# Attention and routed feed-forward on one core: routing's small operands and q's norms move to PSUM, first squares to ScalarE, whole dense chunks, and a tail written out by hand

## The chip, the cores and the metric

The kernel runs on one core of a Trainium2 chip. The metric is the device time of one execution in microseconds (us). The core has TensorE (PE in the profile; its weight loads are PEld), VectorE (DVE), ScalarE (ACT), GpSimd (POOL) and SyncE (SP), which run their own instruction streams and wait for one another by semaphores. Tiles lie in SBUF or in PSUM, the memory into which TensorE's results go; PSUM has eight banks of 2 KB in each partition here.

## What is computed

Attention with RMS-normalised q and k over 8 batches, 12 heads, 448 tokens and 64 channels; its result, seen as 3584 tokens of 768 channels, goes through a dense feed-forward layer and, added to it, one of eight expert layers, chosen per token by the largest gate logit and weighted by its probability.

```python
q_n, k_n = (rmsnorm(q, g_q), rmsnorm(k, g_k))       # x / sqrt(mean(x*x) + 1e-6) * g
attn = np.exp(scores)                               # scores = q_n k_n^T / 8, less the row's maximum
attn = attn / (np.sum(attn, axis=-1, keepdims=True) + 1e-09)
return np.matmul(attn, v).astype(np.float32)
...
h_dense = np.maximum(x @ w1_dense, 0.0)
y_dense = h_dense @ w2_dense
logits = x @ w_gate
expert_idx = np.argmax(logits, axis=1)
...
    h = np.maximum(x[mask] @ w1[e], 0.0)
    y_moe[mask] = gate_w[mask, None] * (h @ w2[e])
return (y_dense + y_moe).astype(np.float32)
```

## The kernel before

The program has two phases. The first (up to L478) does attention, routing and the first dense layer; the second (from L480) gathers tokens by expert and does the rest in 35 tiles of up to 128 tokens.

In the first phase the 96 heads go in 24 groups of four, three groups to a batch. `load` (SP queue) fetches q and k of a group, `load_v` (POOL queue) fetches v of two groups. `squares` (L183, POOL) squares q and k, `sums` (L188, DVE) adds over the channels, `norms` (L194, ACT) makes mean squares into reciprocal roots by Ln and Exp, `normalise` (L200) multiplies, q on DVE and k on POOL, `transposes` (L208, PE) and `turned` (L216, DVE) bring them channel-first. `scores` (L226) does four matmuls and one large Exp on ACT, seven times a group; the Exp's results lie in the tail of the expert weights' tile `we`, so the last weights load late. `attend` (L240) multiplies by v, 28 small matmuls for each of four steps, `divide` (L256, DVE) normalises into `xa`, `xtrans` (L265, PE) and `xturned` (L275, DVE) transpose that into `xT`.

Per batch, routing follows: `logits` (L279, PE), `choose` (L288, DVE: maximum, differences `cent`, the first maximal expert as `hot` and one-hot `oh`; ACT's Exp; the gate value; stores to `records`, a DRAM tensor with one row per token), `ranks` (L313, PE: how many earlier tokens chose each expert), and `places` (L325, DVE): it adds the counts so far, keeps the chosen expert's number in `rf`, splits it in whole tiles `tj` and rest `lo` through int32 and a shift (L335 to L338), and makes the selection matrix `sel`. The first dense layer is made in chunks of six matmuls of 512 columns, one chunk for 128 tokens: `fill` (L437) issues them a few at a time, `dense` (L346) writes a bank `ff`, `relu` (L356, ACT) empties it into `hd` and SP stores that to `records`. `hd` has one buffer.

PSUM: two buffers of two banks for scores, and four one-bank buffers that `tr`, `av`, `xt`, `lp`, `rk` and `ff` take in turn, in the order in which the program asks for them.

The order of the instructions on PE, POOL, SP, DVE and ACT is that of the code (`manual_schedule`, L447). `period(g)` (L370) is one turn: around the seven scores of group g+1 it puts the attention of group g, the normalising and transposing of group g+2 and the squares, sums and norms of group g+3; the transposes of x of group g-1 at the end; and, when a batch's second group is under way, the routing of the batch before. Weights go out on POOL's queue at a pace (`LATE`, `WPACE`, at i == 2).

After the loop come the rest of the dense chunks, then the second phase's table of slots on DVE (L490 to L550: `tl` compares slot numbers with tile numbers, `val` multiplies by token numbers), 32 matmuls `slp` (L517), and the first gathers (L555).

Of the kernel before, what the change touches and what calls it, by code (L numbers as in the profile page):

```python
# [9 lines left out]
F32 = mybir.dt.float32  # L10
BF16 = mybir.dt.bfloat16
# [7 lines left out]
def kernel(  # L19
# [71 lines left out]
    lo = const.tile([P, B, 4], BF16)  # L91
# [6 lines left out]
    LATE, WPACE = 8, 2.6  # L98
# [36 lines left out]
    with tc.tile_pool(name="a_ld", bufs=2) as ld, \  # L135
# [3 lines left out]
        xin, sqs, ssqs, rs, xn, qkT, exs, xas, xTs, avs, trs = [{} for _ in range(11)]  # L139
# [41 lines left out]
        def squares(g, name):  # L181
            for hh in range(2):
                sqs[name, g, hh] = sb.tile([P, J * D], F32, tag="sq", name="sq", bufs=3)  # L183
                x = xin[name, g][:, hh]
                nc.gpsimd.tensor_mul(sqs[name, g, hh], x, x)  # L185
# [14 lines left out]
        def normalise(g, name):  # L200
            eng = nc.vector if name == "q" else nc.gpsimd
# [63 lines left out]
        def xtrans(g):  # L265
            b, gb = divmod(g, NPR // GP)
            ps = wkp.tile([P, GP, S], BF16, tag="wk", name="xt")
# [5 lines left out]
            trs["x"] = ps  # L273

        def xturned(g):  # L275
            b, gb = divmod(g, NPR // GP)
            nc.vector.tensor_copy(xTs[b][:, gb * GP:(gb + 1) * GP], trs["x"])  # L277

        def logits(b):  # L279

            lp = wkp.tile([P, 4, E], F32, tag="wk", name="lp")
# [4 lines left out]
            trs["l"] = lp  # L286

        def choose(b):  # L288
            lp = trs["l"]
            mx = sb.tile([P, 4, 1], F32, tag="mx")  # L290
            nc.vector.tensor_reduce(mx, lp, AX.X, ALU.max)
            cent = sb.tile([P, 4, E], F32, tag="cent")
            nc.vector.tensor_sub(cent, lp, mx.to_broadcast([P, 4, E]))

            hot = sb.tile([P, 4, E], F32, tag="hot")
# [8 lines left out]
            nc.scalar.activation(eg, cent, AF.Exp)  # L304
            sm = sb.tile([P, 4, 1], F32, tag="sm")
            nc.vector.tensor_reduce(sm, eg, AX.X, ALU.add)
# [6 lines left out]
        def ranks(b):  # L313

            rk = wkp.tile([P, 5, E], F32, tag="wk", name="rk")
# [7 lines left out]
            trs["r"] = rk  # L323

        def places(b):  # L325
            rk = trs["r"]
            c0, c1 = counts[b % 2], counts[1 - b % 2]
            rr = sb.tile([P, 4, E], F32, tag="rr")
# [3 lines left out]
            rf = sb.tile([P, 4], F32, tag="rf")  # L332
# [332 lines left out]
```

## Time and profile before

| | |
|---|---|
| timed runs | 501.01, 504.06, 504.98 us |
| profiled execution | 500.06 us |
| its span in the trace | 498.4 us |
| busy PE | 398.2 us (80%), mean granted clock 0.912 |
| busy DVE | 299.1 us (60%) |
| busy POOL | 263.4 us (53%) |
| busy ACT | 234.4 us (47%) |
| read from HBM | 74.90 MB |

The span goes from the first to the last instruction; the execution's own time has 1.66 us around it. The busy shares are means over two phases that differ much: in the first DVE, POOL and ACT carry most of their work, in the second PE runs almost without a break. A line Lnnn is a line of the kernel; `y<-xq,r 128x448 bf16<-128x448 f32` is the output tile, the inputs, and their partitions, elements and types; a bracket such as `[0.82 <-ACT hd L360]` is the idle time of that engine before the row and the instruction that ended it.

### The profile page before, as it was taken

Reading aid. Unit: us, or ns where it says so; the run is one execution under the profiler, and the core shown is the slowest. Engines: PE = TensorE matmul, PEld = TensorE weight load, DVE = VectorE, ACT = ScalarE, POOL = GpSimd, SP = SyncE. Lnnn points to the kernel's source line nnn. Section 1 sums busy time; section 2 is a strip of 40 time slices with the busy share of each in tenths; the row PEclk is TensorE's granted clock in tenths of the full one; section 3 lists DMA queues with packets and bytes.
Section 4 is the critical chain, followed back from the end, with each engine's and each line's share of the span. In section 5 each row is a group of like instructions: output and inputs, shape, how many; then the busy total and the mean of one; then the engine's idle time right before and its main releaser. Section 6 shows DMA issues by size and latency. Waiting matters only on the chain.

```text
span 498.4 us, 13956 instructions
## 1 busy us (share of the span) xinstructions
PE 398.2 (80%) x5628; PEld 241.8 (49%) x5628; DVE 299.1 (60%) x747; ACT 234.4 (47%) x362; POOL 263.4 (53%) x285
## 2 busy tenths in 40 slices
PE   0448787878979859788788862499999999999994
PEld 0135463544535536545455521346666666666662
DVE  3569899998998989998984515213323323323320
ACT  1437774765846847758567102023333333333331
POOL 8689994774784947659742200304434434434422
PEclk9999897997989989989888857569999999999999
DMA  8949767498393973945649994414453454454430
GB/s 217 243 110 260 149 184 156 131 254 169 99 228 114 189 200 94 283 117 130 140 84 154 232 215 124 117 36 151 128 182 128 132 180 137 135 169 165 143 121 1
DMA packets 50303, 77.24 MB, mean 155 GB/s; under 512 B 8573, under 2 KB 46205, under 8 KB 50240
## 3 DMA queue, kind: packets, MB, share of 16 engines
q0 software_dynamic: 24544, 43.31, 39.6%
q1 hardware_dynamic: 25376, 33.04, 20.9%
q8 instruction: 46, 0.75, 0.6%
q14 instruction: 17, 0.14, 0.1%
q10 hardware_dynamic: 320, 0.00, 0.0%
HBM read 74.90 MB, written 23.86 MB: 198 GB/s over the span
## 4 chain that ended last, share of the span: by engine, by line
issue 30%; DVE 30%; POOL 14%; PE 13%; DMA 9%; ACT 2%; POOLq 1%; ACTq 0%; SPq 0%; DVEq 0%
DMA records<-hd 7%; POOL xg L555 7%; DVE ssq L190 6%; DVE xa L262 5%; PE av L253 5%; DVE y L204 4%; POOL sq L185 3%; PE sc L235 3%; POOL out_dram L609 3%; PE ff L351 3%; DVE y L221 2%; DVE xT L277 2%; DVE lo L338 2%; ACT hd L360 2%; DMA gk<-in_g_k_dram 1%
## 5 line engine op out<-in xcount | busy, mean ns | idle before, releaser
L238 ACT ACTIVATE we<-sc 128x896 bf16<-128x896 f32 x168 | 147.1, 919 | 63.9 <-PE sc L235 63.3
L609 POOL DMA_INDIRECT out_dram<-ys,dest x35 | 35.5, 1014 | 97.9 <-ACT ys L608 97.9
L253 PE MATMUL av<-va,we 64*128 64x65 bf16 x2688 | 68.0, 197 | 16.5 <-DVE xT L277 10.0
L235 PE MATMUL sc<-y 64*64 64x448 bf16 x672 | 69.5, 411 | 12.8 <-ACT we L238 11.4
L204 POOL TENSOR_TENSOR y<-xk,r 128x448 bf16<-128x448 f32 x48 | 52.3, 1110 | 41.4 <-ACT r L197 41.4
L253 PEld LDWEIGHTS <-we 64*128 64x128 bf16 x2688 | 53.1, 98 | 42.0 <-issue 38.7
L351 PE MATMUL ff<-wd,xT 128*128 128x512 bf16 x192 | 59.1, 449 | 12.6 <-DVE xa L262 9.3
L589 ACT COPY heT<-hp 128x512 bf16<-128x512 bf16 x35 | 20.5, 585 | 92.4 <-PE hp L587 89.7
L607 DVE COPY ys<-yp 128x384 f32<-128x384 f32 x35 | 19.5, 557 | 72.7 <-issue 55.7
L185 POOL TENSOR_TENSOR sq<-xk 128x448 f32<-128x448 f32 x48 | 44.2, 936 | 31.9 <-DVE ssq L190 31.6
L190 DVE TENSOR_REDUCE ssq<-sq 128x7 f32<-128x448 f32 x96 | 56.0, 609 | 4.5 <-POOL sq L185 4.3
L555 POOL DMA_INDIRECT xg<-records,row x35 | 34.2, 977 | 43.6 <-DVE t L543 32.4
L577 PE MATMUL he<-we,xT 128*128 (+1 forms) x210 | 53.6, 393 | 0.2 <-issue 0.2
L596 PE MATMUL yp<-wd,hdT 128*128 128x384 bf16 x280 | 51.2, 326 | 1.1 <-ACT ys L608 1.1
L566 DVE COPY xT<-xp 128x768 bf16<-128x768 bf16 x35 | 19.5, 557 | 53.4 <-PE he L577 30.0
L601 PE MATMUL yp<-we,heT 128*128 (+1 forms) x280 | 51.2, 326 | 0.0
L185 POOL TENSOR_TENSOR sq<-xq 128x448 f32<-128x448 f32 x48 | 49.0, 1041 | 0.0
L204 DVE TENSOR_TENSOR y<-xq,r 128x448 bf16<-128x448 f32 x48 | 46.0, 998 | 4.8 <-ACT r L197 4.8
L213 PE MATMUL tr<-ident,y 128*128 128x128 bf16 x336 | 27.3, 239 | 27.0 <-DVE y L204 22.2
L262 DVE TENSOR_TENSOR xa<-av,inv 128x256 bf16<-128x256 f32 x96 | 40.7, 424 | 3.3
L235 PEld LDWEIGHTS <-y 64*64 64x64 bf16 x672 | 20.9, 107 | 40.0 <-issue 30.6
L213 PEld LDWEIGHTS <-y 128*128 128x128 bf16 x336 | 22.5, 108 | 33.7 <-DVE y L204 23.9
(101 smaller groups left out, 497.8 us busy)
## 6 DMA issues: line engine op xcount, KB each, us to landing
we<-in_moe_w_dram POOLq DMA_DIRECT2D x16, 768.0 KB
xq<-in_q_dram SPq DMA_DIRECT2D x25, 448.0 KB, 4.2
xk<-in_k_dram SPq DMA_DIRECT2D x25, 448.0 KB, 5.2
xv<-in_v_dram POOLq DMA_DIRECT2D x11, 448.0 KB
records<-xa SPq DMA_DIRECT2D x8, 576.0 KB, 7.2
records<-hd SPq DMA_DIRECT2D x24, 128.0 KB, 1.8
wd<-in_moe_w_dense_dram POOLq DMA_DIRECT2D x2, 768.0 KB
records<-xa SPq DMA_DIRECT2D x8, 96.0 KB, 7.7
```

The lines of the kernel that those rows point to most:

```text
L185: nc.gpsimd.tensor_mul(sqs[name, g, hh], x, x)
L190: nc.vector.tensor_reduce(ssqs[g][:, "qk".index(name), hh], sqs[name, g, hh].rearrange("p (j d) -> p j d", d=D), AX.X, ALU.add)
L204: eng.tensor_mul(y[:, :, hh], xin[name, g][:, hh].rearrange("p (j d) -> p j d", d=D), rs[g][:, "qk".index(name), hh].unsqueeze(2) .to_broa ...
L235: nc.tensor.matmul(ps[r * D:(r + 1) * D, hh, :S], kT[rows, r, j], qT[rows, r].rearrange("p j s -> p (j s)"), start=True, stop=True)
L238: nc.scalar.activation(x, ps[:, :, :S], AF.Exp, scale=scale)
L253: nc.tensor.matmul(avs[hh, r][:, m], exs[g, j][rows, hh, QC[m]:QC[m] + P], va[rows, hh, j, :De], start=(j == 0), stop=(j == J - 1))
L262: nc.vector.tensor_mul(xas[b][:, :, h * D:(h + 1) * D], avs[hh, r][:, :, :D], inv.to_broadcast([P, 4, D]))
L351: nc.tensor.matmul(ff[0], xTs[b][:, kk, QC[m]:QC[m] + P], wd1[:, kk], start=(kk == 0), stop=(kk == KD - 1))
L555: nc.gpsimd.indirect_dma_start(out=xg, out_offset=None, in_=rec, in_offset=bass.IndirectOffsetOnAxis(ap=row[:, t:t + 1], axis=0))
L577: nc.tensor.matmul(he, xTs[t][:, kk], we[:, bass.ds(eregs[t], 1), 0, kk * F:(kk + 1) * F] .rearrange("p o f -> p (o f)"), start=(kk == 0), ...
L596: nc.tensor.matmul(yp[:, dd, :HD], hdTs[t][:, i], wd2[:, i, dd * HD:(dd + 1) * HD], start=(i == 0), stop=False)
L601: nc.tensor.matmul(yp[:, dd, :HD], heTs[t][:, i], we[:, bass.ds(eregs[t], 1), 1, i * Dm + dd * HD:i * Dm + (dd + 1) * HD] .rearrange("p o ...
```

## The change

- `hot`, `cent` and, in `places`, `rr`, `rf` and `lo` are no longer SBUF tiles but unused columns of the PSUM bank of `lp` or `rk`. The int32 chain becomes float arithmetic: `tj` is rounded by adding and subtracting 12582912, one instruction less.
- `norms` is one Ln and two Exps; k's norms go to SBUF, q's to the spare end of the bank that the transposes of x (`xt`) fill. `norms` now takes that bank; `xtrans` moves from the end of a period (group g-1) to i == 0 of the next (g-2), and `xturned` from i == 0 to i == 1.
- The gate value and the stores leave `choose` for a function `gates`, called after `ranks`.
- `fill` issues six matmuls, a whole chunk, instead of five, and `hd` has two buffers.
- At the start ACT squares the first two groups, DVE normalises the first group's k too, and `constants` and the first three weight loads stand after the squares of the third group. In the loop `LATE` goes from 8 to 5 and `WPACE` from 2.6 to 2.1; the last weight is loaded in the second phase, at t == 0.
- The loop runs 24 periods; its two last ones are written out, with the last batch's dense chunks between `choose` and `ranks`, and between `places` and the slot matmuls. `tl` and `val` are made in two halves.

```diff
-    LATE, WPACE = 8, 2.6
+    LATE, WPACE = 5, 2.1
...
+                if scalar:
+                    nc.scalar.activation(sqs[name, g, hh], x, AF.Square)
+                else:
+                    nc.gpsimd.tensor_mul(sqs[name, g, hh], x, x)
...
-            r = sb.tile([P, 2, 2, J], F32, tag="r", name="r")
-            nc.scalar.activation(r, ssqs[g], AF.Ln, bias=eps_t, scale=1.0 / D)
-            nc.scalar.activation(r, r, AF.Exp, scale=-0.5)
-            rs[g] = r
...
+            ln = sb.tile([P, 2, 2, J], F32, tag="ln", name="ln")
+            nc.scalar.activation(ln, ssqs[g], AF.Ln, bias=eps_t, scale=1.0 / D)
+            trs["x"] = wkp.tile([P, 1024], BF16, tag="wk", name="xt")
+            rs["q", g] = trs["x"][:, GP * S:].bitcast(F32)[:, :2 * J].rearrange(
+                "p (h j) -> p h j", h=2)
+            rs["k", g] = sb.tile([P, 2, J], F32, tag="r", name="r")
+            for n, name in enumerate("qk"):
+                nc.scalar.activation(rs[name, g], ln[:, n], AF.Exp, scale=-0.5)
...
-                               rs[g][:, "qk".index(name), hh].unsqueeze(2)
-                               .to_broadcast([P, J, D]))
+                               rs[name, g][:, hh].unsqueeze(2).to_broadcast([P, J, D]))
...
-            lp = trs["l"]
+            ws = trs["w"]
+            lp, hot, cent = [ws[:, i * 4 * E:(i + 1) * 4 * E].rearrange("p (m e) -> p m e", e=E)
+                             for i in range(3)]
...
-            cent = sb.tile([P, 4, E], F32, tag="cent")
...
-            hot = sb.tile([P, 4, E], F32, tag="hot")
...
+            rr = ws[:, 64:64 + 4 * E].rearrange("p (m e) -> p m e", e=E)
+            rf, lof = ws[:, 128:132], ws[:, 132:136]
...
-            ri = sb.tile([P, 4], I32, tag="ri")
-            nc.vector.tensor_copy(ri, rf)
-            nc.vector.tensor_scalar(ri, ri, 7, None, op0=ALU.arith_shift_right)
-            nc.vector.tensor_copy(tj[:, b], ri)
-            nc.vector.scalar_tensor_tensor(lo[:, b], in0=tj[:, b], scalar=-float(P), in1=rf,
+
+            nc.vector.tensor_scalar(lof, rf, 63.5, 1.0 / P, op0=ALU.subtract, op1=ALU.mult)
+            nc.vector.tensor_scalar(tj[:, b], lof, 12582912.0, 12582912.0, op0=ALU.add,
+                                    op1=ALU.subtract)
+            nc.vector.scalar_tensor_tensor(lof, in0=tj[:, b], scalar=-float(P), in1=rf,
...
-                hd = sb.tile([P, F], BF16, tag="hd", bufs=1)
+                hd = sb.tile([P, F], BF16, tag="hd", bufs=2)
...
-                        xturned(g - 2)
+                        xtrans(g - 2)
...
-                        fill(g, 5)
+                        fill(g, KD)
...
+                    if g > 1:
+                        xturned(g - 2)
...
-                    if g > 0 and g - 1 < NG:
-                        xtrans(g - 1)
                     if gb == 1 and g > 1:
                         ranks(b - 1)
+                        gates(b - 1)
                         places(b - 1)
-                    fill(g, 5)
+                    fill(g, KD)
...
-                constants()
                 setup()
+                for name in "qk":
+                    squares(0, name, scalar=True)
...
+                for name in "qk":
+                    normalise(0, name, nc.vector)
+                    transposes(0, name)
...
+                for name in "qk":
+                    squares(1, name, scalar=True)
...
+                for j in range(J):
+                    scores(0, j)
+                    if j == 1:
+                        norms(1)
+                        for name in "qk":
+                            normalise(1, name)
+                        squares(2, "q")
...
                 for job in wjobs[:3]:
                     nc.gpsimd.dma_start(*job)
...
+                constants()
+                norms(2)
...
+                xtrans(NG - 2)
+                xturned(NG - 2)
+                fill(NG, KD)
                 relu()
-                fill(10 ** 6, 10 ** 6)
+                xtrans(NG - 1)
+                xturned(NG - 1)
+                logits(B - 1)
+                choose(B - 1)
+                fill(NG + 1, 12)
                 relu()
-                while nw[0] < len(wjobs):
+                ranks(B - 1)
+                gates(B - 1)
+                places(B - 1)
+                fill(NG + 1, 12)
+                relu()
+                while nw[0] < len(wjobs) - 1:
...
+                if t == 0:
+                    nc.gpsimd.dma_start(*wjobs[-1])
```

Three places show how instructions stand now. The first is DVE at the end of a period with routing: `places` and what follows it, with the engines and queues that a row waits for. Before:

```order
L329 TENSOR_TENSOR rr<-rk,counts_90 128x32 [waits PE_49]
L330 TENSOR_TENSOR counts_89<-rk,counts_90 128x8
L331 TENSOR_TENSOR rr<-rr,oh 128x32 [waits DVE_49]
L333 TENSOR_REDUCE rf<-rr 128x4 [waits DVE_49]
L335 CAST ri<-rf 128x4 [waits DVE_49]
L336 TENSOR_SCALAR ri<-ri 128x4 [waits DVE_49]
L337 CAST tj<-ri 128x4 [waits DVE_49]
L338 SCALAR_TENSOR_TENSOR lo<-tj,rf 128x4 [waits DVE_49]
L340 TENSOR_TENSOR sel<-iop,lo 128x512 [waits DVE_49]
L277 COPY xT<-xt 128x896
L204 TENSOR_TENSOR y<-xq,r 128x7x64 [waits DMAHW3_49,Activation_49]
```

Of the change, the same place (`rk` names every tile that shares the bank, `xt` the bank in which q's norms lie):

```order
L344 TENSOR_TENSOR rk<-rk,counts_89 128x32 [waits PE_49]
L345 TENSOR_TENSOR counts_88<-rk,counts_89 128x8 [waits DVE_49]
L346 TENSOR_TENSOR rk<-rk,oh 128x32 [waits DVE_49]
L347 TENSOR_REDUCE rk<-rk 128x4 [waits DVE_49]
L349 TENSOR_SCALAR rk<-rk 128x4 [waits DVE_49]
L350 TENSOR_SCALAR tj<-rk 128x4 [waits DVE_49]
L352 SCALAR_TENSOR_TENSOR rk<-tj,rk 128x4 [waits DVE_49]
L354 TENSOR_TENSOR sel<-iop,rk 128x512 [waits DVE_49]
L211 TENSOR_TENSOR y<-xq,xt 128x7x64 [waits DMAHW2_49,PE_49,Activation_49]
...
L285 COPY xT<-xt 128x896
```

One instruction is gone, the copy of x's transposes stands behind q's multiplication instead of ahead of it, and that multiplication now waits for PE as well.

The second place is POOL's queue from its first instructions on. Before:

```order
L105 AFFINE_SELECT tri<-ones 128x128
L108 IOTA iop 128x128
...
L115 IOTA pp 64x1 x2
L123 IOTA iot_82 128x1120
L453 DMA wgb<-in_moe_w_gate_dram 128x6x8
L453 DMA wd_92<-in_moe_w_dense_dram 128x6x512
L453 DMA wd_93<-in_moe_w_dense_dram 128x4x768
L185 TENSOR_TENSOR sq<-xq 128x448 x2
L185 TENSOR_TENSOR sq<-xk 128x448 x2
L204 TENSOR_TENSOR y<-xk,r 128x7x64 x2
```

Of the change:

```order
L177 COPY va_110<-xv 128x14x64
L211 TENSOR_TENSOR y<-xk,r 128x7x64 x2
L187 TENSOR_TENSOR sq<-xq 128x448 x2
L187 TENSOR_TENSOR sq<-xk 128x448 x2
L177 COPY va_111<-xv 128x14x64
L498 DMA wgb<-in_moe_w_gate_dram 128x6x8
L498 DMA wd_91<-in_moe_w_dense_dram 128x6x512
L498 DMA wd_92<-in_moe_w_dense_dram 128x4x768
L104 AFFINE_SELECT tri<-ones 128x128
...
L114 IOTA pp 64x1 x2
L122 IOTA iot_82 128x1120
```

The constants and the three loads have gone behind the first k that POOL normalises (that of the second group), the squares of the third group and two copies of v.

The third place is PE behind the last batch's logits: the end of those, and what stands there next. Before:

```order
L284 LDWEIGHTS xT
L284 MATMUL lp<-wgb,xT 128x8
L320 LDWEIGHTS tri
L320 MATMUL rk<-oh,tri 128x32
L320 LDWEIGHTS ones
L320 MATMUL rk<-oh,ones 128x24
```

Of the change:

```order
L293 LDWEIGHTS xT
L293 MATMUL lp<-wgb,xT 128x8
L365 LDWEIGHTS xT
L365 MATMUL ff<-wd_91,xT 128x512
...
L334 LDWEIGHTS tri
L334 MATMUL rk<-oh,tri 128x32
L334 LDWEIGHTS ones
L334 MATMUL rk<-oh,ones 128x24
```

Twelve dense matmuls, two chunks, now stand between the logits and the ranks; twelve more stand between the ranks and the slot matmuls, where there were 24.

## Rows read from the trace of the kernel before

**Rows 1.** Stretch: us, busy PE (x) PEld DVE ACT POOL, PEclk, DMA, GB/s.
```profile
170.00:204.00 34.00, 26.58 (x544) 16.61 (x543) 31.07 (x69) 22.12 (x34) 22.33 (x25) 0.90 0.71 172
```

**Rows 2.** Timeline, DVE, three dense periods: start us, us, engine line op tile, xcount.
```profile
168.62 1.89 DVE L204 TENSOR_TENSOR y<-xq,r 128x448 bf16<-128x448 f32 x2
...
174.14 0.75 DVE L296 SCALAR_TENSOR_TENSOR hot<-cent,prio 128x32 f32<-128x32 f32 x1
...
178.73 0.62 DVE L335 CAST ri<-rf 128x4 int32<-128x4 f32 x1
...
181.16 1.70 DVE L338 SCALAR_TENSOR_TENSOR lo<-tj,rf 128x4 bf16<-128x4 f32 x1
...
184.03 1.15 DVE L204 TENSOR_TENSOR y<-xq,r 128x448 bf16<-128x448 f32 x2
...
201.78 2.37 DVE L204 TENSOR_TENSOR y<-xq,r 128x448 bf16<-128x448 f32 x2
```

**Rows 3.** Timeline, DVE, the routing in the last periods, where POOL rests.
```profile
272.86 0.19 DVE L296 SCALAR_TENSOR_TENSOR hot<-cent,prio 128x32 f32<-128x32 f32 x1
...
277.56 0.17 DVE L335 CAST ri<-rf 128x4 int32<-128x4 f32 x1
277.77 0.17 DVE L336 TENSOR_SCALAR ri<-ri 128x4 int32<-128x4 int32 x1
```

**Rows 4.** Groups by line, whole span: busy us, mean ns | idle us before.
```profile
L204 DVE TENSOR_TENSOR y<-xq,r 128x448 bf16<-128x448 f32 x48 | 46.0, 998 | 4.8 <-ACT r L197 4.8
...
L262 DVE TENSOR_TENSOR xa<-av,inv 128x256 bf16<-128x256 f32 x96 | 40.7, 424 | 3.3
...
L329 DVE TENSOR_TENSOR rr<-rk,counts 128x32 f32<-128x32 f32 x8 | 1.4, 178 | 0.5 <-PE rk L320 0.5
```

**Rows 5.** Timeline, DVE, q's multiplication where stretches begin or end.
```profile
34.22 1.90 DVE L204 TENSOR_TENSOR y<-xq,r 128x448 bf16<-128x448 f32 x2 [0.64 <-ACT r L197]
...
68.14 1.89 DVE L204 TENSOR_TENSOR y<-xq,r 128x448 bf16<-128x448 f32 x2
...
258.72 2.37 DVE L204 TENSOR_TENSOR y<-xq,r 128x448 bf16<-128x448 f32 x2
```

**Rows 6.** Timeline, PE, the first of the last periods.
```profile
255.96 0.61 PE L253 MATMUL av<-va,we 64*128 64x65 bf16 x28
256.50 0.38 PE L235 MATMUL sc<-y 64*64 64x448 bf16 x4
256.82 0.62 PE L270 MATMUL xt<-ident,xa 128*128 128x128 bf16 x8
...
258.85 1.25 PE L351 MATMUL ff<-wd,xT 128*128 128x512 bf16 x5
...
263.02 0.94 PE L213 MATMUL tr<-ident,y 128*128 128x128 bf16 x14 [0.82 <-ACT hd L360]
```

**Rows 7.** Timeline, ACT, the norms' Exp in a dense period.
```profile
177.19 0.23 ACT L197 ACTIVATE r<-r 128x28 f32<-128x28 f32 x1
```

**Rows 8.** Timeline, all engines, the start; in brackets the wait and its releaser.
```profile
8.32 1.85 POOL L185 TENSOR_TENSOR sq<-xq 128x448 f32<-128x448 f32 x2
...
10.31 0.77 DVE L69 TENSOR_TENSOR gqk<-gq,gk 128x1 f32<-128x1 f32 x1 [7.05 <-DMA gk<-in_g_k_dram]
...
18.90 0.96 PE L235 MATMUL sc<-y 64*64 64x448 bf16 x8 [0.72 <-DVE y L223]
```

**Rows 9.** Timeline, all engines, end of attention to the first gather.
```profile
281.32 1.05 PE L253 MATMUL av<-va,we 64*128 64x65 bf16 x55 [0.70 <-DVE xa L262]
...
300.25 0.16 DVE L329 TENSOR_TENSOR rr<-rk,counts 128x32 f32<-128x32 f32 x1
...
304.85 1.39 DVE L513 TENSOR_TENSOR val<-tl,tok 128x1120 bf16<-128x1120 bf16 x2
...
310.79 4.00 PE L517 MATMUL slp<-val,sel 128*128 128x70 bf16 x32 [8.20 <-ACT hd L360]
...
316.76 1.07 POOL L555 DMA_INDIRECT xg<-records,row  x1 [32.41 <-DVE t L543]
```

More of the change, by code (lines that the diff above doesn't have):

```diff
@@ L138 @@
          tc.tile_pool(name="a_wk", bufs=4, space=bass.MemoryType.PSUM) as wkp:
[L139 removed]
+        xin, sqs, ssqs, rs, xn, qkT, exs, xas, xTs, avs, trs, xps = [{} for _ in range(12)]
         gt = sb.tile([P, 4, RC - GO], F32, name="gt", tag="gt", bufs=1)
@@ L449, in run @@
                 load(2)
-                constants()
                 setup()
+                for name in "qk":
+                    squares(0, name, scalar=True)
+                    for hh in range(2):
+                        sums(0, name, hh)
+                norms(0)
+                for name in "qk":
+                    normalise(0, name, nc.vector)
+                    transposes(0, name)
+                for name in "qk":
+                    turned(0, name)
+                values(0)
@@ new lines, in run @@
+                for name in "qk":
+                    squares(1, name, scalar=True)
+                    for hh in range(2):
+                        sums(1, name, hh)
+                for j in range(J):
+                    scores(0, j)
+                    if j == 1:
+                        norms(1)
+                        for name in "qk":
+                            normalise(1, name)
+                        squares(2, "q")
+                for name in "qk":
+                    transposes(1, name)
+                    turned(1, name)
@@ L452, in run @@
+                for hh in range(2):
+                    sums(2, "q", hh)
+                squares(2, "k")
+                values(1)
+                for hh in range(2):
+                    sums(2, "k", hh)
                 for job in wjobs[:3]:
                     nc.gpsimd.dma_start(*job)
-                for g in range(3):
-                    for name in "qk":
-                        squares(g, name)
-                        for hh in range(2):
-                            sums(g, name, hh)
-                    norms(g)
-                    if g < 2:
-                        for name in "qk":
-                            normalise(g, name)
-                            transposes(g, name)
-                            turned(g, name)
-                        values(g)
-                    if g == 0:
-                        for j in range(J):
-                            scores(0, j)
-                    load(g + 3)
+                constants()
@@ L470, in run @@
+                norms(2)
                 load_v(1)
-                for g in range(NG + 2):
+                for g in range(3, 5):
+                    load(g)
+                for g in range(NG):
                     period(g)
+                xtrans(NG - 2)
+                xturned(NG - 2)
+                fill(NG, KD)
                 relu()
-                fill(10 ** 6, 10 ** 6)
-                relu()
-                while nw[0] < len(wjobs):
+                xtrans(NG - 1)
+                xturned(NG - 1)
```

48 lines of the change are left out of this document (26 added, 22 removed).

## The prediction

> **What bounds the kernel now.** I read the table of busy time by stretch first. In the dense part of the attention loop VectorE (DVE) works 31.07 of 34 us in 69 instructions; with the few tens of ns between two instructions that is a full engine, while ScalarE (ACT) and GpSimd (POOL) stand at 22 us and TensorE (PE) at 26.58, at a granted clock of 0.90 [rows 1]. So a microsecond taken from DVE counts there until PE is full.
>
> Next I read DVE's own timeline over three periods, 168.62 to 201.78 [rows 2]. It is 33.16 us; the first period, which holds the routing of a batch, takes 15.41 (168.62 to 184.03), the two others 17.75 together. In the routing period tiny instructions take absurdly long: `hot` on 32 elements 0.75 us, and the chain from the CAST at 178.73 to the end of `lo` at 182.86 takes 4.13 us for four instructions on 4 elements. The same instructions, when POOL has no elementwise work left, take 0.19 and 0.17 us, one every 0.21 us [rows 3]. So their price is not their own. What the slow ones share is that everything they touch lies in SBUF; `rr` at L329, which reads the matmul's result in PSUM, averages 0.178 us over all batches, POOL busy or not [rows 4]. q's multiplication by its norms (L204) shows it at a larger size: the pair takes 1.15 us at 184.03 and 1.89 or 2.37 in other periods, with a mean of 0.998 us for one [rows 2, 4]. I read this as DVE waiting for POOL over a path to SBUF that both use.
>
> I cut the span into stretches by the pair's starts: up to 34.22; then four periods without routing to 68.14 (33.9); then 17 periods, six of them with routing, to 258.72 (190.6) [rows 5]; to the end of the last attention matmul, 281.32 plus 1.05 (23.7); from there to the first gather at 316.76 (34.4) [rows 9]; and 181.6 of expert tiles to the end of the span at 498.4, in which nothing but one weight load changes.
>
> **The dense periods.** Removed from DVE in a routing period: `hot` 0.75 to 0.19 is 0.56; the four instructions of 4.13 become three at 0.21, so 3.50 [rows 2, 3]. In every period q's pair goes from 2.00 (twice 0.998) to the undisturbed 1.15, so 0.85; three periods 2.55 [rows 2, 4]. Together 6.6 us, and 33.2 becomes 26.6. The price of a PSUM operand rests on rows: 256 elements from PSUM take 424 ns at L262, 448 undisturbed ones 575 at 184.03, in step with the added elements, and L329 is at 0.178 [rows 2, 4]. A write by DVE or ACT into PSUM has no row; below it is bounded by no difference, above by doubling the 0.2 us of some eight small instructions, 1.6 us in three periods, nearest to nothing since the reads cost nothing.
>
> [...]
>
> Not all 6.6 us arrive. PE's work for three periods, by starts and durations at the full clock [rows 6]: 28 attention matmuls every 0.54 (255.96 to 256.50), four times a period; four scores matmuls 0.32 (256.50 to 256.82), seven times; eight transposes 0.62; fourteen 0.94; a dense chunk of six 1.50 (five in 1.25). That is 5.96 a period and four chunks, 23.9, plus logits and ranks, about 25. And two new waits come in. First, q's norms lie in the bank that the transposes of x fill, those transposes stand ahead of the multiplication, and the order shows the multiplication waiting for PE where it did not. In a period whose end has a chunk, PE does that chunk, four scores matmuls and eight transposes first, 2.4 us, and DVE has two divisions to cover 1.3 of it: about 1 us, once in three periods, since the routing covers another and the third has no chunk. Second, a further Exp for the norms, 0.23 us in each period [rows 7], which delays POOL's k: 0.7 in three. So I take 26.6 + 1.0 + 0.7 = 28.3, and for 17 periods 160.4 instead of 190.6: **30.2 less**. Bounds: 6.6 arrives whole, 37; PE and its waits keep three periods at 30.5, 18.
>
> The whole chunks remove a bank held across two periods by a half-made chunk. Its wait goes into the same three periods and is not counted again. The weights' earlier pace costs POOL the issue of three more loads inside the loop, while it has 12 of 34 us free [rows 1]; if that cover were gone, the 1.07 us of a gather's issue [rows 9], the nearest row, would make it 3.2.
>
> **The four early periods.** These have no routing and no dense work. They lose 0.85 on DVE and gain the Exp, 0.23: four times about 0.65, **2.6 less**. Bounds 0 and 4.
>
> **The start.** POOL's first square begins at 8.32 because constants and three weight loads stand ahead [rows 8]; now ACT squares. But DVE's third instruction in the new order after the first two sums is `gqk`, which waited for its load until 10.31 and held DVE to about 11.0. Behind it: two sums 1.1, norms 0.8, four multiplications at 0.58 are 2.3, transposes and copies of k 1.6: scores at 16.8 instead of 18.90, 2.1 less. Then the moved work comes back: three loads and the constants, about 5 us of POOL, now stand between the squares of the third group and its k, and DVE waits in `constants` for POOL's `pp`. What the second group gains from its earlier norms (they no longer stand behind seven exponentials) is 5.7 for me, so this stretch gains nothing to speak of and the start **1.5 less**. Bounds: 6 less, if `gqk`'s load lands early, and 2 more.
>
> **The end of attention.** The last 23.7 us have one routing, with POOL idle, so the undisturbed price already: two q pairs **1.5 less**. Then, now, PE waits 8.2 us for ACT's `hd` before the slot matmuls, because `hd` has one buffer and each store has to land first; the whole stretch is 34.4 [rows 9]. After: two chunks, sixteen transposes and logits about 5; six choosing instructions 1.3, with two chunks (3.0) beside them; ranks 0.5: `rr` at 8.5. From `rr` to the end of `val` it took 6.0 (300.25 to 306.24), so 14.5. The slot matmuls take 4.0, half of them now before `val` is whole, and 2.0 passes to the gather (314.79 to 316.76): 19. If the matmuls still wait for the last `hd`, whose stores now go in pairs, it is 23. I take 21: **13.4 less**. Bounds 10 and 17.
>
> **The sum.** 1.5 + 2.6 + 30.2 + 1.5 + 13.4 = 49.2; 498.4 becomes 449.2, and with the 1.66 us around the span (500.06) 450.9. The median of the three timed runs is 4.0 above that profiled execution, so I write **452**.
>
> **Rivals.**
> 1. *DVE's gain arrives whole.* For it: PE runs at 0.90 of its clock now and would have fewer long waits. 37 instead of 30.2, 4 in the early periods, 17 at the end: about 440. Against it: the new wait on PE.
> 2. *PE and the shared banks become the bound.* For it: PE has 25 us of work in three periods and does it in order. Three periods at 30.5: 18 less instead of 30.2, and 10 at the end: about 467.
> 3. *The PSUM operands do not free DVE*, since the wait belongs to the output or to POOL itself. Then only start and end remain, 16.4 less: about 485. L329 speaks against it [rows 4], but it writes SBUF, and the new ones write PSUM.
> 4. *Slower.* PE's transposes of x now stand behind the norms of the group three ahead, which come from POOL's squares over DVE's sums and ACT. If the norms are late by w, PE, and all scores after it, lose w in each of 24 periods; the gain is gone at w = 2.1 us. Against it: the norms of a period end now at 177.42 [rows 7], before `places` comes to its CAST at 178.73 [rows 2], and PE's transposes come only after the next period's first scores.
>
> **How the numbers follow.** The forecast, 443 to 463, has a chance of 0.55; rival 1 (434 to 443) 0.13; rival 2 (463 to 476) 0.20; rival 3 0.06; rival 4 0.03, and 0.03 for a change that ends within 1% because small waits eat it. A difference within 1% is about what a measurement of this kernel cannot tell from no change. The range 436 to 474 leaves out rivals 3 and 4 and the ends of 1 and 2. Faster 0.94, same 0.03, slower 0.03.
>
> **What would show it.** In the changed kernel: q's pair at 1.15 us in all periods and the instructions of `places` at 0.2, with POOL busy beside them; three dense periods at 28 us; DVE idle before q's pair waiting for PE's `xt`, about 1 us in one period of three; scores starting near 17; 21 us from the last attention matmul to the first gather. I am wrong if the pair stays at 2 us (rival 3), if PE's waits grow in place of DVE's work (rival 2), or if the waits for `hd` stay as long with two buffers.

## The result, and the profile after

The changed kernel takes 456.73 us (median of four runs, 455.86 to 458.04) against 503.7 before: a ratio of 0.9076, 95% interval 0.9033 to 0.9119. Its profiled execution took 458.04 us with a span of 456.3, 42.1 less than the 498.4 before. The stretches are cut as in the prediction, at the start of q's multiplication, at the end of the last attention matmul, and at the first gather:

| stretch | before | after | difference | forecast |
|---|---|---|---|---|
| start, up to the third group | 34.22 | 30.79 | -3.4 | -1.5 |
| four early periods | 33.92 | 39.95 | **+6.0** | -2.6 |
| seventeen dense periods | 190.58 | 163.84 | -26.7 | -30.2 |
| to the last attention matmul | 23.65 | 21.42 | -2.2 | -1.5 |
| to the first gather | 34.39 | 21.24 | -13.1 | -13.4 |
| expert tiles | 181.64 | 179.06 | -2.6 | 0 |

The timeline of the changed kernel in a dense period with routing (start us, us, engine line op tile; in brackets the wait and its releaser) answers [rows 2]:

```profile
163.28 0.20 DVE L305 SCALAR_TENSOR_TENSOR lp<-lp,prio 128x32 f32<-128x32 f32 x1
...
166.40 1.83 POOL L211 TENSOR_TENSOR y<-xk,r 128x448 bf16<-128x448 f32 x2 [2.80 <-ACT r L205]
...
167.31 0.17 DVE L349 TENSOR_SCALAR rk<-rk 128x4 f32<-128x4 f32 x1
...
167.51 0.16 DVE L350 TENSOR_SCALAR tj<-rk 128x4 f32<-128x4 f32 x1
...
167.71 0.17 DVE L352 SCALAR_TENSOR_TENSOR rk<-tj,rk 128x4 f32<-128x4 f32 x1
...
176.31 1.83 POOL L211 TENSOR_TENSOR y<-xk,r 128x448 bf16<-128x448 f32 x2 [1.60 <-ACT r L205]
...
176.85 1.15 DVE L211 TENSOR_TENSOR y<-xq,xt 128x448 bf16<-128x448 f32 x2 [0.23 <-PE xt L278]
```

The `places` chain runs at 0.16 to 0.17 us an instruction beside a busy POOL, and q's pair takes 1.15 us while POOL multiplies k. The groups by line over the whole span (busy us, mean ns | idle before, releasers) say the same for all 48, and show the two new waits:

```profile
L211 DVE TENSOR_TENSOR y<-xq,xt 128x448 bf16<-128x448 f32 x48 | 27.6, 617 | 9.1 <-PE xt L278 6.8 <-ACT xt L205 1.7 <-PE sc L241 0.6
...
L278 PE MATMUL xt<-ident,xa 128*128 128x128 bf16 x192 | 15.9, 230 | 12.2 <-ACT xt L205 11.4
```

998 ns have become 617 [rows 4], and the busy time of the group 27.6 us instead of 46.0; DVE waits 6.8 us for the transposes of x, and PE 11.4 us for the norms that lie in their bank.

Where the early periods lost, the timeline shows POOL waiting:

```profile
27.68 1.58 POOL L498 DMA_DIRECT2D wd<-in_moe_w_dense_dram  x2
...
31.76 0.78 POOL L171 DMA_DIRECT2D xv<-in_v_dram  x1
...
44.35 0.93 POOL L177 COPY va<-xv 128x896 bf16<-128x896 bf16 x1 [5.58 <-DMA xv<-in_v_dram]
```

The load of v for groups 2 and 3 is issued 4 us behind the dense layer's weights on the same queue and lands 12.6 us after its issue; `values` waits 5.58 us for it, and the squares and the k of the next groups stand behind.

At the end (timeline, answering [rows 9]) the slot matmuls wait 2.05 us for `hd` where they waited 8.20:

```profile
267.12 1.09 ACT L374 ACTIVATE hd<-ff 128x512 bf16<-128x512 f32 x2 [4.64 <-DMA records<-hd]
...
268.58 1.52 DVE L561 TENSOR_TENSOR val<-tl,tok 128x560 bf16<-128x560 bf16 x4
...
271.27 4.00 PE L565 MATMUL slp<-val,sel 128*128 128x70 bf16 x32 [2.05 <-ACT hd L374]
...
277.24 1.05 POOL L603 DMA_INDIRECT xg<-records,row  x1 [20.01 <-DVE t L591]
```

The tiles, in which nothing was meant to change, gained 2.6 us. The table by stretch (us, busy PE (x) PEld DVE ACT POOL, granted clock, DMA share, GB/s) of their first 20 us, before and then after:

```profile
316.76:336.76 20.00, 13.52 (x75) 7.66 (x76) 3.53 (x9) 2.93 (x5) 4.93 (x5) 0.61 0.31 92
```
```profile
277.24:297.24 20.00, 14.08 (x96) 8.38 (x97) 4.43 (x11) 3.61 (x6) 7.81 (x8) 0.76 0.61 151
```

The granted clock is 0.61 there before and 0.76 after; 75 against 96 matmuls get done. In pieces of 5 us it is 0.50, 0.50, 0.50 and 0.93 before, and 0.50, 0.55, 1.00 and 1.00 after: it rises from 0.50 about 5 us earlier. The stretch ahead of the tiles is shorter after the change, 21.2 us instead of 34.4, but its length is not what decides. With one buffer and five matmuls at a time (an experiment below) that stretch takes 32.09 us, and the same 20 us have a clock of 0.76 and all the tiles 179.15 us; with routing's operands back in SBUF it takes 20.02 us, and they have 0.65 and 180.47:

```profile
302.65:322.65 20.00, 13.80 (x94) 8.39 (x97) 4.43 (x11) 3.61 (x6) 7.80 (x8) 0.76 0.58 151
```
```profile
286.13:306.13 20.00, 14.13 (x87) 8.08 (x88) 4.29 (x11) 3.62 (x6) 6.81 (x7) 0.65 0.55 131
```

The time of the tiles goes with the clock; why the clock rises when it does stays open.

Executions that took over 1.5% more than the fastest of the same kernel are left out of the times of the experiments below, and the profiles of the two variants that move the constants are of such executions, so that their stretches are compared only where the clock is named.

### The profile page after: what moved, and what is told of

It is laid out like the page before. It is cut to its first block, busy times and chain, and to the rows that moved or that the text cites. A ratio compares the mean times of both kernels' runs of the same rounds, so it can differ in the third digit from the quotient of the medians.

```text
span 456.3 us, 13950 instructions
## 1 busy us (share of the span) xinstructions
PE 384.7 (84%) x5628; PEld 239.3 (52%) x5628; DVE 255.7 (56%) x744; ACT 238.8 (52%) x394; POOL 240.6 (53%) x275
## 4 chain that ended last, share of the span: by engine, by line
issue 32%; DVE 21%; PE 21%; POOL 16%; ACT 4%; DMA 4%; POOLq 1%; ACTq 0%; DVEq 0%
DVE ssq L192 8%; PE ff L365 8%; POOL xg L603 7%; PE av L259 5%; DVE xa L268 4%; PE sc L241 3%; PE xt L278 3%; POOL out_dram L657 3%; POOL sq L187 3%; DVE y L227 2%; DVE y L229 2%; DMA records<-hd 2%; ACT we L244 2%; DVE y L211 2%; DMA gk<-in_g_k_dram 2%
## 5 line engine op out<-in xcount | busy, mean ns | idle before, releaser
L259 PE MATMUL av<-va,we 64*128 64x65 bf16 x2688 | 63.9, 198 | 4.4 <-issue 3.5
L259 PEld LDWEIGHTS <-we 64*128 64x128 bf16 x2688 | 51.4, 99 | 26.4 <-issue 23.2
L211 POOL TENSOR_TENSOR y<-xk,r 128x448 bf16<-128x448 f32 x46 | 42.1, 937 | 41.7 <-ACT r L205 41.7
L365 PE MATMUL ff<-wd,xT 128*128 128x512 bf16 x192 | 52.1, 413 | 8.3 <-DVE xa L268 5.6
L625 PE MATMUL he<-we,xT 128*128 (+1 forms) x210 | 52.3, 386 | 0.5 <-issue 0.5
L187 POOL TENSOR_TENSOR sq<-xk 128x448 f32<-128x448 f32 x44 | 40.7, 938 | 16.8 <-DVE ssq L192 16.7
L187 POOL TENSOR_TENSOR sq<-xq 128x448 f32<-128x448 f32 x44 | 40.1, 932 | 0.0
L630 ACT ACTIVATE hs<-he,xg 128x512 bf16<-128x512 f32 x35 | 24.0, 687 | 27.8 <-PE he L625 18.1
L241 PEld LDWEIGHTS <-y 64*64 64x64 bf16 x672 | 20.5, 107 | 32.9 <-issue 22.9
L649 PEld LDWEIGHTS <-heT 128*128 128x128 bf16 x280 | 27.4, 98 | 18.1
```

The source lines that it names most:

```text
L241: nc.tensor.matmul(ps[r * D:(r + 1) * D, hh, :S], kT[rows, r, j], qT[rows, r].rearrange("p j s -> p (j s)"), start=True, stop=True)
L259: nc.tensor.matmul(avs[hh, r][:, m], exs[g, j][rows, hh, QC[m]:QC[m] + P], va[rows, hh, j, :De], start=(j == 0), stop=(j == J - 1))
L365: nc.tensor.matmul(ff[0], xTs[b][:, kk, QC[m]:QC[m] + P], wd1[:, kk], start=(kk == 0), stop=(kk == KD - 1))
L625: nc.tensor.matmul(he, xTs[t][:, kk], we[:, bass.ds(eregs[t], 1), 0, kk * F:(kk + 1) * F] .rearrange("p o f -> p (o f)"), start=(kk == 0), ...
L649: nc.tensor.matmul(yp[:, dd, :HD], heTs[t][:, i], we[:, bass.ds(eregs[t], 1), 1, i * Dm + dd * HD:i * Dm + (dd + 1) * HD] .rearrange("p o ...
```

## The experiments

All times below are medians, and the ratios are to runs of the kernel before on the same chip. Differences between experiments are read from ratios or from the stretches of their profiles.

**The base.** The changed kernel again, unchanged.

> The changed kernel itself, as the common base for the runs beside it. All theories: 456 to 458 us, ratio to the kernel before 0.905 to 0.912; q's pair 1.15 us in every period, 39.9 us for the four early periods, 8.7 us for a dense period without routing.

457.15 us, ratio 0.9084 (0.9027 to 0.9141); early periods 39.49, dense 164.59, end 20.00. The experiments of its group are set against it.

**q's norms back in SBUF.**

```diff
-            rs["q", g] = trs["x"][:, GP * S:].bitcast(F32)[:, :2 * J].rearrange(
-                "p (h j) -> p h j", h=2)
+            rs["q", g] = sb.tile([P, 2, J], F32, tag="rq", name="rq")
```

> q's norms go back to an SBUF tile; the xt bank is still taken by norms at the same place, so only the operand's place and the wait on that bank change. Theory A (a VectorE operation with two SBUF inputs lasts until the GpSimd instruction beside it ends): q's pair takes 1.9 to 2.4 us again wherever GpSimd multiplies k beside it, DVE gains 0.85 to 1.2 us of work in each of 21 periods, 18 to 25 us, of which the waits for PE's xt and ACT's norms that fall away (6.8 us on DVE, 11.4 us on PE in the changed kernel) give some back: 463 to 475 us. Rival B (PE is the bound in the changed kernel, DVE has 10 per cent free): the pair gets slower, but the time stays at 455 to 460 us. Rival C (the place of the operand doesn't matter): the pair stays at 1.15 us and the time falls by the waits, to 445 to 455 us.

465.23 us, ratio 0.9254 (0.9196 to 0.9311): 8 us slower, theory A. The group of q's multiplication, and one pair with POOL beside it in the timeline:

```profile
L210 DVE TENSOR_TENSOR y<-xq,rq 128x448 bf16<-128x448 f32 x48 | 51.8, 1120 | 2.8 <-ACT rq L204 2.7
```
```profile
190.94 2.21 POOL L210 TENSOR_TENSOR y<-xk,r 128x448 bf16<-128x448 f32 x2 [1.60 <-ACT r L204]
191.18 2.46 DVE L210 TENSOR_TENSOR y<-xq,rq 128x448 bf16<-128x448 f32 x2
193.12 2.20 POOL L187 TENSOR_TENSOR sq<-xq 128x448 f32<-128x448 f32 x2
```

The pair takes 2.46 us, and POOL's pair 2.21 instead of 1.83: each holds the other up, though the pair ends at 193.64, 0.49 us behind POOL's and not with it as theory A has it. DVE's work grew by 24.2 us (51.8 less 27.6), of which a third reaches the end; its waits before the pair fell from 9.1 us to 2.8, which covers a part.

**Routing's operands back in SBUF, the rounding kept in float.**

```diff
-            lp, hot, cent = [ws[:, i * 4 * E:(i + 1) * 4 * E].rearrange("p (m e) -> p m e", e=E)
-                             for i in range(3)]
+            lp = ws[:, :4 * E].rearrange("p (m e) -> p m e", e=E)
+            hot = sb.tile([P, 4, E], F32, tag="hot")
+            cent = sb.tile([P, 4, E], F32, tag="cent")
...
-            rr = ws[:, 64:64 + 4 * E].rearrange("p (m e) -> p m e", e=E)
-            rf, lof = ws[:, 128:132], ws[:, 132:136]
+            rr = sb.tile([P, 4, E], F32, tag="rr")
+            rf = sb.tile([P, 4], F32, tag="rf")
+            lof = sb.tile([P, 4], F32, tag="lof")
```

> hot, cent, rr, rf and the rest lof go back to SBUF tiles; the float rounding stays, so int32 plays no part. Theory A: hot 0.75 us or more, rr*oh about 0.45, the two tensor_scalar operations and the scalar_tensor_tensor 0.6 to 0.9 each where GpSimd is busy, and each ends when a GpSimd instruction ends; 2.5 to 4 us in each of six dense routing periods, 15 to 24 us of DVE work, and 465 to 478 us. Rival B (PE is the bound): the operations get slower, the time 457 to 462 us. Rival D (the int32 conversions were the slow part, not the place): all stay near 0.2 us and the time at 456 to 458 us.

468.47 us, ratio 0.9305 (0.9237 to 0.9373): 11 us slower, theory A. Not the int32 type but the place makes them slow, and the timeline shows what they wait for:

```profile
172.15 1.83 POOL L211 TENSOR_TENSOR y<-xk,r 128x448 bf16<-128x448 f32 x2 [2.46 <-ACT r L205]
173.39 0.62 DVE L351 TENSOR_SCALAR lof<-rf 128x4 f32<-128x4 f32 x1
173.94 1.82 POOL L187 TENSOR_TENSOR sq<-xq 128x448 f32<-128x448 f32 x2
174.04 0.85 DVE L352 TENSOR_SCALAR tj<-lof 128x4 f32<-128x4 f32 x1
174.93 0.85 DVE L354 SCALAR_TENSOR_TENSOR lof<-tj,rf 128x4 f32<-128x4 f32 x1
```

The same stands in the trace of the kernel before, where POOL's rows beside the chain are:

```profile
177.49 1.83 POOL L204 TENSOR_TENSOR y<-xk,r 128x448 bf16<-128x448 f32 x2 [2.65 <-ACT r L197]
...
181.88 0.94 POOL L185 TENSOR_TENSOR sq<-xk 128x448 f32<-128x448 f32 x1
```

They end at 179.32 and 182.82, the CAST and `lo` at 179.35 and 182.86 [rows 2]. In the run here POOL's pair ends at 173.98, DVE's first instruction at 174.01; POOL's two squares end at about 174.87 and 175.76, DVE's next two at 174.89 and 175.78. Each of these instructions on four elements lasts until the POOL instruction beside it is over, within 0.03 us here and 0.04 us before. In the last routing of the same run, with POOL idle, the same three take 0.15 to 0.17 us. `sums`, a reduction with one SBUF input, keep 0.61 us beside POOL (at 166.74, where POOL's two pairs of squares, 1.82 us each, begin at 165.22 and 167.00). What parts them from the TENSOR_SCALAR instructions here, which have one SBUF input too, no run shows.

**v loaded ahead of the weights.**

```diff
                 values(1)
+                load_v(1)
...
                 constants()
                 norms(2)
-                load_v(1)
```

> The load of v for groups 2 and 3 is issued ahead of the gate's and the dense layer's weights instead of behind them and the constants. Theory A (the early periods lost 6 us because GpSimd waits 5.6 us for v behind 3 MB of weights): the wait of values for xv goes, the fifth period shrinks from 13.1 to about 8.7 us, and the time to 450 to 453 us. Rival B (the DMA queues are full there, so whatever comes last is waited for): the wait moves to q, k or the weights, and the time stays at 455 to 458 us.

453.70 us, ratio 0.9049 (0.8978 to 0.9120), which the base's interval overlaps; the mechanism shows in the profile. Of POOL's two waits for v (11.7 us in the base) the one in the early periods is gone and the one at the start, 6.2 us, is left. The four early periods (table by stretch) take 32.86 us instead of 39.49:

```profile
32.00:64.86 32.86, 24.73 (x576) 16.75 (x576) 27.30 (x68) 23.96 (x37) 29.02 (x33) 0.95 0.97 214
```

This is 1.1 us less than before the change, and 7.1 less than the 39.95 of the changed kernel's first profile, at nearly the same clock (0.95 and 0.96; the base's was 0.83 there). Theory A by the profile; the time lies between the two theories.

**One buffer for `hd`.**

```diff
-                hd = sb.tile([P, F], BF16, tag="hd", bufs=2)
+                hd = sb.tile([P, F], BF16, tag="hd", bufs=1)
```

> hd has one buffer again, all else as changed. Theory A (the end of attention was long because each relu waits for the store of the one before): from the last attention matmul to the first gather 28 to 32 us instead of 20 to 21, PE waiting for ACT's hd again; in the dense loop two chunks of a period follow each other by 2 to 3 us, so a store of 2 to 4 us is met there too, some us more: 466 to 474 us. Rival B (the end got short because the dense chunks stand inside the routing waits): the end 22 to 24 us, 459 to 461 us.

493.37 us, ratio 0.9783 (0.9702 to 0.9864): 35 us slower, twice to four times what theory A said and far from B. The end takes 25.55 us, 5.6 more than the base, and the stretch ahead of it 27.55, 11.3 more together; but the dense periods take 188.71, nearly what they took before the change. One of them in the timeline (SP's rows are the stores), and ScalarE's group over the whole span:

```profile
125.32 0.60 ACT L374 ACTIVATE hd<-ff 128x512 bf16<-128x512 f32 x1 [1.23 <-DMA records<-hd]
125.94 5.41 SPq L377 DMA_DIRECT2D records<-hd  x2
...
130.27 0.60 ACT L374 ACTIVATE hd<-ff 128x512 bf16<-128x512 f32 x1 [3.55 <-DMA records<-hd]
130.92 0.91 PE L219 MATMUL tr<-ident,y 128*128 128x128 bf16 x7 [2.68 <-ACT hd L374]
```
```profile
L374 ACT ACTIVATE hd<-ff 128x512 bf16<-128x512 f32 x32 | 19.0, 595 | 48.3 <-DMA records<-hd 42.6 <-PE ff L365 5.2
```

The second relu of a period waits 3.55 us for the first one's store, at the head of ScalarE's queue, ahead of the Exp that PE needs; PE stands 2.68 us for the bank.

**Three buffers for `hd`.** `bufs=3` in the same line.

> hd has three buffers. Theory A: the waits of ACT for the stores at the end (4.6 and 1.9 us before the last two pairs) lose one store's length, PE's last chunk no longer waits 2.7 us for a bank, and the slot matmuls start when val is there, 1.5 to 2.5 us earlier: 454.5 to 456 us. Rival B (the stores queue behind the last weights, so a third buffer only moves the wait): 456 to 458 us.

459.56 us, ratio 0.9183 (0.9114 to 0.9253): no gain, above both theories and nearest to rival B; the interval overlaps the base's. The end took 19.41 us in its profile, 0.6 less than the base, and the dense periods 165.98.

**The last dense chunks all behind `places`.**

```diff
                 choose(B - 1)
-                fill(NG + 1, 12)
-                relu()
                 ranks(B - 1)
                 gates(B - 1)
                 places(B - 1)
-                fill(NG + 1, 12)
+                fill(NG + 1, 24)
                 relu()
```

> The last batch's four dense chunks all stand behind places, ahead of the slot matmuls; none between choose and ranks. Theory A (the second buffer made the end short, the order adds little): the first gather comes 0 to 2 us later, 457 to 459 us. Rival B (the interleaving made it short): PE idles through choose (1.3 us) and places, the two chunks add their 3 us and their stores behind them, 4 to 6 us later: 461 to 463 us.

460.16 us, ratio 0.9202 (0.9114 to 0.9291). The time lies between the two theories, and its interval reaches the base's: it decides nothing. In the profile the end takes 22.55 us, 1.3 to 2.6 more than in the two profiles of the changed kernel, which is nearer to theory A's size. Of the 16.2 us by which the last two stretches of attention are shorter in the base than before (58.0 to 41.8), the buffer's 11.3 are thus the greater part; of the end alone (34.4 to 20.0), the buffer and the order together give back some 7 to 8 of its 14.4 us, and no run here shows the rest.

**Five matmuls at a time.** `fill(g, 5)` in both places of the loop, the last `fill` taking what is left.

> In the loop fill issues five dense matmuls at a time again, so that a chunk is begun in one period and ended in the next and holds one of four banks across it; the tail takes what is left. Theory A (a held bank costs waits on the other three): 2 to 3 us in three periods, 468 to 475 us, with PE or ACT waiting for a bank (idle of PE before tr or av, released by ACT's hd or by DVE). Rival B (four banks do): 456 to 459 us.

472.38 us, ratio 0.9408 (0.9350 to 0.9466): theory A, 16 us by the ratios. The dense periods take 175.69 us, 11.1 more than the base. PE's waits between 70 and 240 us (total, times, longest) are for DVE to empty a bank:

```profile
PE av L259 <- DVE y L227: 6.7, 14, 0.6
PE ff L365 <- DVE xa L268: 6.5, 9, 1.2
PE av L259 <- DVE xT L285: 4.9, 10, 0.9
```

The base has 1.0 and 5.8 us for the first two and none for the third. DVE waits 11.8 us for `xt` there, 4.4 in the base, and ScalarE 41.6 us for scores, 30.5 in the base. The edit holds a bank across two periods and also moves dense matmuls from one place to another; no run parts the two.

**q's norms in a bank of their own.**

```diff
-            trs["x"] = wkp.tile([P, 1024], BF16, tag="wk", name="xt")
-            rs["q", g] = trs["x"][:, GP * S:].bitcast(F32)[:, :2 * J].rearrange(
+            rs["q", g] = wkp.tile([P, 512], F32, tag="wk", name="nq")[:, :2 * J].rearrange(
                 "p (h j) -> p h j", h=2)
...
-            if g + 4 >= NG:
+            if True:
                 trs["x"] = wkp.tile([P, 1024], BF16, tag="wk", name="xt")
```

> q's norms lie in a PSUM bank of their own, asked for by norms; the transposes of x ask for theirs when they start. Nothing else changes; VectorE's multiplication of q then waits for ScalarE alone and the transposes no longer for the norms. Theory A (the shared bank costs the waits seen in the changed kernel, 11 us of PE for ACT's xt and 7 us of DVE for PE's xt, which partly lie in one another): q's pair still 1.15 us, both waits gone, 449 to 454 us. Rival B (a fifth user of four banks makes PE wait for a bank elsewhere: tr, av or ff released later): the waits come back under other names, 456 to 465 us.

457.31 us, ratio 0.9138 (0.9096 to 0.9180): rival B, no gain. Both waits went (q's pair now idles 2.1 us for ACT, PE's transposes 0.7 us), and came back elsewhere. DVE's longest wait between 70 and 240 us, and PE's two longest:

```profile
DVE inv L265 <- PE av L258: 23.3, 12, 2.5
```
```profile
PE ff L364 <- DVE xa L267: 6.7, 5, 1.5
PE av L258 <- DVE xa L267: 2.7, 7, 0.4
```

DVE waits for PE's attention 23.3 us instead of the base's 17.6. PE and DVE wait for each other around the same loop, and what was taken out of it here came back at other places of it.

**Constants and weights later, and into POOL's idle time.** Two variants; the diff is the second's. In the first the three weight loads and GpSimd's constants follow the first period, VectorE's share the second; in the second GpSimd's constants stand where it waits at the start, and v is loaded ahead of the weights.

```diff
                 values(0)
+                constants()
...
+                load_v(1)
                 for job in wjobs[:3]:
                     nc.gpsimd.dma_start(*job)
-                constants()
                 norms(2)
-                load_v(1)
...
                     period(g)
+                    if g == 1:
+                        tokens()
```

> Behind the squares and norms of the third group come v's load and the first period; the three first weight loads and GpSimd's constants follow the first period, VectorE's share of them the second; the three fills that need no GpSimd go to the very start. Theory A (the early periods lose to what stands ahead of v and of group 2's k on GpSimd's queue, and VectorE's wait of 2.5 us for GpSimd's iota): the wait for v as in the run with v early gone, the first period's start at 28 to 29.5 us instead of 31.2, the four early periods 33 to 35 us: 447 to 452 us. Rival B (GpSimd is the bound of the early periods, 29.8 of 39.5 us busy, so moved work only comes back later): 453 to 456 us.

> GpSimd's constants go to where GpSimd waits at the start (idle from 10 to 19 us in the changed kernel, behind the first copy of v); v for groups 2 and 3 is loaded ahead of the three first weights, which stay ahead of the first period; VectorE's token numbers follow the second period. Theory A (the early periods are bound by GpSimd's queue, so only work moved into its idle time is gained): the first period's start at 27.5 to 28.5 us instead of 31.2, the four early periods 31.5 to 33.5 us, together 3 us less than with v early alone, 449 to 452 us. Rival B (the gain is lost again at the dense periods, whose pace is another's): 453 to 457 us.

The first: 450.65 us, the mean of 448.59 and 452.70, ratio 0.9000 (0.8929 to 0.9072). That is theory A's range, but on two executions that lie 4 us apart, and the interval overlaps the base's. The first period starts at 27.76, but POOL's 5 us of moved work stand ahead of group 3's k (35.15 to 40.1), and PE waits 2.86 us for it. The second: 449.21 us, ratio 0.8967 (0.8917 to 0.9016), by the ratios 6 us below the changed kernel and clear of its interval. Theory A for the time: it beats both kernels. Not for the stretches, in which the clock is 0.95 as in the run with v early: the early periods take 35.83 us (31.5 to 33.5 expected), and the dense periods begin at 63.43, 1.4 us before those of that run and not 3.

**One buffer and five at a time.** The two edits of before together, in the changed kernel.

> One buffer for hd and chunks issued five matmuls at a time, both as before the change; all else as changed. Undone alone the buffer costs 36 us and the whole chunks 15 us. Theory A (the one buffer costs so much because whole chunks come twice in a period, so that each second relu waits for a store on ScalarE's queue, ahead of the Exp that PE needs): with split chunks the relus of a period stand further apart, and both together cost less than the buffer alone, 475 to 488 us. Rival B (the two costs are separate and add up): 505 to 510 us.

484.41 us, ratio 0.9671 (0.9613 to 0.9730): theory A. With both undone the dense periods take 179.41 us, 9.3 less than with the buffer alone, and only 3.7 more than with the pieces alone (175.69). One buffer is bearable in this kernel where chunks are cut in pieces, and very dear where two whole ones come in a period (24.1 us of the dense periods).

## Why the prediction was right, and where it was not

The time came out 4.7 us above the 452 that was forecast, inside the likeliest case, for mostly the reasons given; one step had the wrong sign, and one gain was put down to the wrong edit. Part of it was luck. As profiled executions, 458.04 us stand against 450.9: the early periods and the dense ones came out 8.6 and 3.5 us worse than forecast, and start, the last stretch of attention and tiles 1.9, 0.7 and 2.6 better, the tiles for a reason that was not thought of. Of the 4.0 us by which the median lay above the profiled execution before, 452 holds only 1.1; after the change the median lies 1.3 below.

- **PSUM operands free DVE.** Right in mechanism, the price a little too high. q's pair takes 1.15 us and the chain 0.17 an instruction, as said. But 2.00, twice the mean duration, counts the time in which the two instructions of a pair overlap. By the busy time of the group a pair went from 1.92 (46.0 by 24) to 1.15 (27.6 by 24), so 0.77 and not 0.85 were freed. The sign I read as "a path to SBUF that both use" was in [rows 2] more sharply than I saw, in the ends of the CAST and of `lo`, which lie within 0.04 us of POOL's; that the operand's place decides is shown, by 1.15 against 2.46 us for a pair beside POOL; the path itself no run shows. A write into PSUM, for which there was no row, costs nothing that shows (0.20 us for `hot` in PSUM, 0.19 in SBUF undisturbed [rows 3]). So the bound of 1.6 us falls. Rival 3 is out by two runs.
- **The dense periods.** -26.7 of -30.2: three periods take 28.9 us (163.84 by 17, times 3), 28.3 were forecast. Most of the difference is a slip in the sum. From 33.2 to 28.3 are 4.9 us in three periods and 27.8 in seventeen; 30.2 came of setting 28.3 against the mean of all of them, 33.6, which is longer than the three that were read. Measured, 33.6 became 28.9, 4.7 less. The wait of 1 us for the shared bank is there (5.2 us between 70 and 240 us, 0.9 in three periods), but without it the time is the same; the 0.7 us for the second Exp no run shows by itself. What bounds these periods, as far as the runs show, is PE and DVE in turn. PE works 101.52 of 114.95 us from 119.63 to 234.58, at a clock of 0.96, DVE 96.77.
- **What the gain hangs on.** "Its wait goes into the same three periods and is not counted again" for the whole chunks, and `hd`'s second buffer counted at the end alone: the runs show that 11.1 and 24.1 us of the dense periods go when either is undone. For the buffer the trace of the kernel before gave no sign. Of ScalarE's waits for a store there (the group over the whole span) 28.8 us lie behind 258 us and only 4.1 in the dense periods:

```profile
L360 ACT ACTIVATE hd<-ff 128x512 bf16<-128x512 f32 x32 | 19.0, 594 | 35.0 <-DMA records<-hd 32.9 <-PE ff L351 2.2
```

  It is the whole chunks that make the second buffer necessary: with chunks in pieces one buffer costs the dense periods 3.7 us, with whole ones 24.1. The sum was right because I set the periods by DVE's and PE's work and assumed that nothing else would hold them; that these two edits make this assumption true I did not see. Undone one at a time, norms, routing, chunks and buffer cost 8, 11, 16 and 35 us, 70 together, against 47 that all gave: they are not terms of a sum.
- **The early periods.** The failed step, 6.0 more where 2.6 less were forecast. I counted what POOL's moved work does to k and to DVE's wait for `pp` (2.52 us), but not the other instruction on that queue: v's load is now behind the weights'. It cost 5.6 us of waiting. With v first the stretch is 32.9, 1.1 less than before, so the step is wrong for v's load in the main. A part is the cut, which goes by q's pair: by the starts of POOL's k the four periods take 37.64 us and, with v first, 31.31, where they took 33.01, so 4.6 more and 1.7 less. The last 0.9 of the forecast 2.6 no run accounts for.
- **The start.** Twice the gain by the stretch, 3.4: scores begin at 15.87 (16.8 forecast), and `gqk` waited until 10.12, as forecast. But the stretch ends with q's pair, which no longer stands beside k's: POOL begins the third group's k at 32.56 instead of 34.28, 1.7 less, about as forecast. The other 1.7 us only pass from this stretch to the early periods.
- **The end.** 13.1 for 13.4, by the chain as worked out: slot matmuls after `hd`, the last wait 2.05 us. What each edit gives of it is shown in part: 5.6 us by the buffer (11.3 with the stretch ahead), 1.3 to 2.6 by the order.
- **The tiles.** 2.6 less where nothing was counted, with the higher clock at their start; what raised it earlier is open.
- **Rivals 2 and 4.** The wait of rival 4 is there, 11.4 us of PE for the norms in its bank, and does not decide: w is 0.5 us a period, below its 2.1, and PE would have waited elsewhere.

## What to carry to other kernels

When a tiny VectorE instruction takes as long as the GpSimd instruction beside it lasts, compare their ends: if they agree, put one operand into PSUM (here q's pair takes 1.15 us so, and 2.46 with both in SBUF and GpSimd beside it), and count the gain by durations that the same line has with GpSimd idle. Before moving work on a queue, list every load that it now stands in front of, not only the computation (here v's, 5.58 us of waiting). An edit that seems to matter only at one place (a second buffer) can be what lets another edit's gain through; undo each alone before calling the gains a sum.

## What was not expected of the hardware

- With routing's operands in SBUF, an instruction on four elements lasted 0.62 to 0.85 us beside GpSimd and 0.15 to 0.17 alone, ending within 0.03 us of GpSimd's instruction; with q's norms in SBUF, GpSimd's multiplication pays too, 2.21 instead of 1.83 us for a pair.
- In the changed kernel, with its whole chunks, the stores of 128 KB from one buffer are met again as 42.6 us of waiting on ScalarE, where two buffers leave 6.8.
- The clock of the first 20 us of the tiles was 0.61 before and 0.65 to 0.76 in the three other runs named above, and the tiles took 181.64, 180.47, 179.15 and 179.06 us in that order. The length of the stretch ahead (34.39, 20.02, 32.09 and 21.24) does not order them.
